# Two transformer layer pairs on one core: longer planned PSUM clears, more PSUM bank sets, and another instruction order

## The chip, the cores and the metric

The kernel runs on one core of one Trainium2 chip. TensorE (PE) multiplies matrices into PSUM, eight banks of 512 fp32 columns on 128 partitions. ScalarE (ACT), VectorE (DVE) and GpSimd (POOL) do the rest, the first two also reading PSUM. SyncE (SP) issues the DMAs. The metric is the device time of one execution in microseconds (us), the median of the runs.

## The reference

One sequence of 2048 tokens, width 512, bf16. Twice in a row, with the same weights, a sliding-window attention layer (32 heads of 16, window 256) and an MLP (512 to 1792 to 512, tanh GELU), each behind a layer norm and with a residual:

```python
def _A_ref(x, wqkv, wo):                       # H = 32, Dh = 16, W = 256
    q, k, v = split((x @ wqkv))                # 32 heads each
    scores = einsum("bhqd,bhkd->bhqk", q, k) * Dh ** -0.5
    mask = (i - j >= 0) & (i - j < W)
    p = softmax(where(mask, scores, -1e9))
    return einsum("bhqk,bhkd->bhqd", p, v) @ wo
def _B_ref(x, w1, b1, w2, b2):
    return gelu(x @ w1 + b1) @ w2 + b2

x = A_x
x = x + _A_ref(_layernorm(x), A_wqkv, A_wo)
x = x + _B_ref(_layernorm(x), B_w1, B_b1, B_w2, B_b2)
x = x + _A_ref(_layernorm(x), A_wqkv, A_wo)
x = x + _B_ref(_layernorm(x), B_w1, B_b1, B_w2, B_b2)
```

## The kernel before

The tokens are 16 tiles of 128; with the two layer pairs there are 32 tile steps (`tau`), grouped by two into 16 attention blocks (`b`) and by two or four into 10 MLP jobs (`J`). All of X and all weights stay in SBUF.

For a tile, `layernorm` takes statistics (`bn_stats`, `bn_aggr`, `veps` on VectorE), the inverse root (`rstd`, a power on GpSimd) and the normalised tile `xn` on VectorE. `xn` has to be transposed. Mostly TensorE does it into PSUM and VectorE or ScalarE copies it out (`xnTA`, `xnTB`). For the MLP's tiles 4 to 29 (`by_dma`) VectorE transposes 32x32 pieces into `xs_` (three buffers), four DMAs write them to a DRAM scratch (`scr_x`), and one DMA reads them back as `xnTB`.

For an attention block, 16-column groups of projections give Q, K and V; the K copy (`KT`) masks odd and even heads. A score visit (`sc`) puts 512 score columns of four row groups into four PSUM banks, two pairs; ScalarE takes the exponential of one pair at a time (128x1024) into the ring `E`. The triangles at the window's two edges are zeroed by a multiplication with `mask01`, on VectorE or GpSimd. A PV group (`pv`, pools name `od`) sums E times V in two banks; VectorE transposes, and divides by the sum of the exponentials (`TT`, `Rc`, `TM`, `OT`). `outproj` adds the result to X.

An MLP job multiplies by W1 into one bank at a time (pool `m1`, for the first six of 14 chunks `o`), applies GELU on ScalarE, and multiplies by W2 (`y`).

PSUM banks come from pools: each kind of user has a list of bank sets, and takes the one that is free first. At the start, 16 matmuls of zeros (`clear`, twice eight banks) precede every other use of PSUM. They read `gT`, which VectorE sets to zero first.

The order of all this isn't written in the program text. Every operation is a node with an engine, a duration, what it reads and writes, and perhaps a second engine that could do it. `ORDER` lists the 3295 nodes in the order in which they are recorded; a negative number picks the node's second engine. `_Plan.follow` walks the list with the nodes' durations, to choose the PSUM banks and to place the waits; each engine then runs its own nodes in that order. So a planned duration emits nothing, and changes only which banks are given out and where a wait stands. The one that the change touches is this:

```python
for h in range(NZ):
    PL.root = (add("pe", clear, 8 * mm(512), reads=["zero", "g0"], writes=["ps:init0", "ps:init1"], prio=-200, geo="f"),)
```

Lines of the profile: L32 and L36 are all matmuls and transposes of TensorE, L861 the memset of the zeros, L844 the reduction for `parmask`, L888 and L893 the loads of X and Wqkv, L933 to L943 the layer norm, L952 to L960 the way through DRAM, L916 and L918 the copies out of PSUM on VectorE and ScalarE, L990 the residual, L1030 the K copy, L1111 the exponential, L1132 the masks, L1197 to L1207 the end of a PV group, L1266 to L1278 the GELU.

Of the kernel before, what the change touches and what calls it, by code (L numbers as in the profile page):

```python
# [518 lines left out]
def bass_interleave_layers__sliding_block__dense_activation_gelu__prompt_kernel(  # L519
# [70 lines left out]
    def mm(n):  # L590
        return n / 2.4 + 2.6

    with ExitStack() as kctx:
        S_ = _Sched(nc, kctx)

        def sb(name, shape, dtype=dt.bfloat16):
# [33 lines left out]
        zero = gT[:, 0, :]  # L630
# [195 lines left out]
        add = PL.add  # L826
# [41 lines left out]
        for h in range(NZ):  # L868
            PL.root = (add("pe", clear, 8 * mm(512), reads=["zero", "g0"], writes=["ps:init0", "ps:init1"], prio=-200, geo="f"),)
# [450 lines left out]
        for i in order:  # L1320
            nd = PL.nodes[i]
            n = 1
            if nd["eng"] == "pe":
                c = _Count()
# [34 lines left out]
```

## Time and profile before

| | us |
|---|---|
| median of 3 runs (lowest, highest) | 461.64 (461.19, 461.93) |
| the profiled execution | 461.4 |
| its span, first to last instruction | 459.7 |
| PE busy | 442.2 |
| ACT busy | 394.2 |
| DVE busy | 370.0 |
| POOL busy | 216.5 |

The profile is of one execution. Its span is what the views divide; 1.7 us of the execution lie around it. The busy times overlap, as the engines run side by side; what ends the kernel is the chain of work in which each step waits for the one before. An idle time in a view has behind it what ended it.

### The profile page before, as it was taken

Reading aid. Unit: us, or ns where it says so; the run is one execution under the profiler, and the core shown is the slowest. Engines: PE = TensorE matmul, PEld = TensorE weight load, DVE = VectorE, ACT = ScalarE, POOL = GpSimd, SP = SyncE. Lnnn points to the kernel's source line nnn. Section 1 sums busy time; section 2 is a strip of 40 time slices with the busy share of each in tenths; the row PEclk is TensorE's granted clock in tenths of the full one; section 3 lists DMA queues with packets and bytes.
Section 4 is the critical chain, followed back from the end, with each engine's and each line's share of the span. In section 5 each row is a group of like instructions: output and inputs, shape, how many; then the busy total and the mean of one; then the engine's idle time right before and its main releaser. Section 6 shows DMA issues by size and latency. Waiting matters only on the chain.

```text
span 459.7 us, 19399 instructions
## 1 busy us (share of the span) xinstructions
PE 442.2 (96%) x8793; PEld 236.5 (51%) x8793; DVE 370.0 (81%) x754; ACT 394.2 (86%) x473; POOL 216.5 (47%) x250
## 2 busy tenths in 40 slices
PE   6987899999889999999999999999999999999997
PEld 3654465754444445555435545546454554454663
DVE  5999878989989688995879988988888968896312
ACT  2999999999989989899996999979997999875442
POOL 4466636712653555553667654462344415451600
PEclk9999999999999999999999999999999999999999
DMA  7670000001020110100030110101030021102011
GB/s 228 206 266 3 4 3 3 5 1 37 8 55 3 20 31 15 37 3 9 16 74 5 27 23 12 40 4 19 3 66 26 6 57 31 43 5 70 13 58 47
DMA packets 27855, 18.17 MB, mean 40 GB/s; under 512 B 15868, under 2 KB 27260, under 8 KB 27772
## 3 DMA queue, kind: packets, MB, share of 16 engines
q1 hardware_dynamic: 27772, 16.92, 13.8%
q8 instruction: 69, 1.13, 1.0%
q14 instruction: 14, 0.11, 0.1%
HBM read 11.41 MB, written 5.51 MB: 37 GB/s over the span
## 4 chain that ended last, share of the span: by engine, by line
PE 70%; ACT 23%; DVE 2%; SPq 1%; DMA 1%; POOL 1%; issue 1%; DVEq 0%; POOLq 0%
PE ps L32 69%; ACT E L1111 18%; ACT gT L1278 2%; PE ps L36 1%; SPq L956 1%; ACT gT L1269 1%; ACT L1111 1%; DMA scr_x<-xs_ 1%; ACT Va L918 1%; ACT QT L918 1%; DVE KT L1030 1%; DVE gT L1266 0%; DMA xnTB<-scr_x 0%; SPq L960 0%; DVE xs_ L952 0%
## 5 line engine op out<-in xcount | busy, mean ns | idle before, releaser
L1111 ACT ACTIVATE E<-ps 128x1024 bf16<-128x1024 f32 x304 | 287.0, 1046 | 26.9 <-PE ps L32 26.3
L1132 POOL TENSOR_TENSOR E<-E,mask 128x512 bf16<-128x512 bf16 (+1 forms) x120 | 125.5, 1059 | 121.6 <-DVE E L1132 43.3
L32 PE MATMUL ps<-W_sb,gT 128*128 128x512 bf16 x448 | 118.3, 380 | 0.0
L32 PE MATMUL ps<-xnTB,W_sb 128*128 128x512 bf16 (+1 forms) x560 | 116.0, 337 | 0.9 <-DMA xnTB<-scr_x 0.7
L990 DVE TENSOR_TENSOR X<-X,ps 128x512 bf16<-128x512 bf16 x64 | 43.5, 683 | 40.3 <-PE ps L32 39.3
L32 PEld LDWEIGHTS ps<-xnTB,W_sb 128*128 128x128 bf16 x560 | 51.2, 98 | 46.0 <-ACT E L1111 2.9
L32 PE MATMUL ps<-QT,KT 32*64 32x320 bf16 (+4 forms) x2976 | 65.4, 258 | 6.6 <-ACT E L1111 4.8
L32 PE MATMUL ps<-xnTA,Wqkv_sb 128*128 128x256 bf16 x512 | 70.1, 274 | 0.7 <-ACT E L1111 0.4
L1278 ACT ACTIVATE gT<-ps,b1T 128x512 bf16<-128x512 f32 (+1 forms) x92 | 48.8, 588 | 22.1 <-PE ps L32 21.6
L940 POOL TENSOR_TENSOR rstd<-veps,mhalf 128x1 f32<-128x1 f32 x64 | 36.5, 575 | 57.0 <-DVE veps L937 55.7
L32 PEld LDWEIGHTS ps<-W_sb,gT 128*128 128x128 bf16 x448 | 39.5, 98 | 42.7 <-issue 5.9
L1132 DVE TENSOR_TENSOR E<-E,mask 128x512 bf16<-128x512 bf16 (+1 forms) x142 | 57.5, 433 | 4.6 <-ACT E L1111 4.5
L32 PEld LDWEIGHTS ps<-xnTA,Wqkv_sb 128*128 128x128 bf16 x512 | 46.0, 98 | 19.3 <-issue 2.9
L32 PEld LDWEIGHTS ps<-QT,KT 32*64 32x64 bf16 x2976 | 27.6, 103 | 51.6 <-ACT E L1111 35.6
L32 PE MATMUL ps<-E,Va 64*17 64x128 bf16 (+3 forms) x3872 | 49.0, 229 | 2.0 <-ACT E L1111 0.7
L1197 DVE STREAM_TRANSPOSE TT<-ps 128x1024 f32<-128x1024 f32 x32 | 39.9, 1245 | 11.6 <-PE ps L32 11.0
L32 PEld LDWEIGHTS ps<-E,Va 64*17 64x17 bf16 x3872 | 39.3, 85 | 19.0 <-PE ps L32 5.4
L1241 POOL TENSOR_TENSOR X<-X,b2b 128x512 bf16<-128x512 bf16 x32 | 36.7, 1157 | 17.9 <-DVE xn L943 6.4
L933 DVE BATCH_NORM_STATS2 stat<-X 128x6 f32<-128x512 bf16 x64 | 43.4, 683 | 1.4 <-DMA X<-in_A_x_dram 0.7
L1030 DVE TENSOR_TENSOR KT<-ps,parmask 128x1024 bf16<-128x1024 f32 x32 | 38.4, 1211 | 3.9 <-PE ps L32 3.7
L1266 DVE TENSOR_SCALAR gT<-ps,b1T 128x512 bf16<-128x512 f32 (+1 forms) x48 | 31.8, 672 | 5.7 <-PE ps L32 5.3
L32 PE MATMUL ps<-Wqkv_sb,xnTA 128*128 128x512 bf16 x128 | 35.2, 381 | 0.2 <-ACT E L1111 0.2
(49 smaller groups left out, 325.2 us busy)
## 6 DMA issues: line engine op xcount, KB each, us to landing
W_sb<-in_B_w_dram SPq DMA_DIRECT2D x2, 1792.0 KB, 12.9
scr_x<-xs_ SPq DMA_DIRECT2D x104, 32.0 KB, 1.6
xnTB<-scr_x SPq DMA_DIRECT2D x26, 128.0 KB, 2.1
out_dram<-X SPq DMA_DIRECT2D x16, 128.0 KB, 1.8
Wqkv_sb<-in_A_wqkv_dram SPq DMA_DIRECT2D x3, 512.0 KB, 6.4
X<-in_A_x_dram SPq DMA_DIRECT2D x3, 512.0 KB, 4.8
X<-in_A_x_dram SPq DMA_DIRECT2D x2, 256.0 KB, 2.9
Wo_sb<-in_A_wo_dram SPq DMA_DIRECT2D x1, 512.0 KB, 6.4
```

The costliest lines, as they stand in the source:

```text
L32: return self.e.matmul(*a, **k)
L918: alt=() if kind not in ACT_OK and not boot else (("act", lambda e, B: e.activation(dst(B), src(B), AF.Copy, scale=1.0), d_act(n) + 14, 0. ...
L933: add("dve", lambda e, B: e.bn_stats(stat6[:, k6, :], X[:, t, :]), 590, reads=["X%d" % t], writes=["st%d" % k6], prio=prio)
L940: add("pool", lambda e, B: e.tensor_tensor(out=rstd[:, k : k + 1], in0=veps[:, k : k + 1], in1=mhalf[:], op=ALU.pow), 535, reads=["ve%d" % ...
L990: add("dve", lambda e, B: e.tensor_tensor(out=X[:, t, :], in0=X[:, t, :], in1=ps[:, B[g][0], :], op=ALU.add), d_psum(512), reads=["X%d" % ...
L1030: add("dve", lambda e, B, g=g, i=i: e.tensor_tensor(out=KT[:, kb, :, 2 * i : 2 * i + 2, :].rearrange("p a c q -> p a (c q)"), in0=ps[:, B[ ...
L1111: add("act", lambda e, B, g_=g_, gi=gi: e.activation(E[:, 2 * gi : 2 * gi + 2, e0 : e0 + 512], ps[:, B[g_][0] : B[g_][0] + 2, :], AF.Exp, ...
L1132: op = lambda e, B, Ew=Ew, Mw=Mw: e.tensor_tensor(out=Ew, in0=Ew, in1=Mw, op=ALU.mult)
L1197: add("dve", lambda e, B: e.transpose(TT[:, s].rearrange("p a c q d -> p (a c q d)"), ps[:, B[g][0] : B[g][0] + 2, :].rearrange("p a n -> ...
L1241: add("pool", lambda e, B: e.tensor_tensor(out=X[:, t, :], in0=X[:, t, :], in1=b2b[:], op=ALU.add), 1110, reads=["X%d" % t, "b2b"], writes ...
L1266: add("dve", lambda e, B, g=g, fc=fc: e.tensor_scalar(out=gT[:, fc, 0:M], in0=ps[:, B[g][0], 0:M], scalar1=b1T[:, fc : fc + 1], scalar2=No ...
L1278: add("act", lambda e, B, g=g, fc=fc: e.activation(gT[:, fc, 0:M], ps[:, B[g][0], 0:M], AF.Gelu_apprx_tanh, bias=b1T[:, fc : fc + 1], scal ...
```

## The change

Five things change in the text. The two clears are planned at 16 and 10 matmul lengths instead of 8 and 8. The score visits may take any two pairs of adjacent banks, also pairs that start at an odd bank; the PV groups likewise. The four writes to the DRAM scratch are planned at 2300 ns with 500 ns of queue instead of 2100 and 400. And `ORDER` is a new list of the same 3295 nodes.

In the new list VectorE's first node is the memset of the zeros, and the `parmask` reduction comes after the fourth `xn`; tile 1's layer norm stands ahead of tile 0's; the first K projection stands ahead of the first Q projection. Of the masks, 31 wide and 8 narrow ones go from VectorE to GpSimd (VectorE then has 91 and 12, GpSimd 127 and 32). One scaling `TM` also goes to GpSimd, and two transposed tiles are copied out by ScalarE instead of VectorE. In the queue of SyncE the four scratch writes of a tile mostly stand together. The numbers of matmuls, DMAs, exponentials and table loads stay.

```diff
         ORDER = [
-            0, 18, 1, 19, 2, 20, 8, 4, 5, 21, 6, 14, 7, 22, 15, 16, 9, 23, 33, 10, 24, 11, 40, 12, 34, 3, 41, 17, 35,
...
+            3276, 3077, 3277, 3278,
         ]
...
         PL = _Plan({
-            "sc": [(0, 1, 2, 3), (4, 5, 0, 1), (2, 3, 4, 5), (6, 7, 0, 1), (2, 3, 6, 7), (4, 5, 6, 7)],
+            "sc": [(0, 1, 2, 3), (4, 5, 0, 1), (2, 3, 4, 5), (6, 7, 0, 1), (2, 3, 6, 7), (4, 5, 6, 7)] + [
+                (a, a + 1, c, c + 1) for a in range(7) for c in range(a + 2, 7) if a % 2 or c % 2],
             "o": [(6,), (7,), (5,), (4,), (3,), (2,), (1,), (0,)],
-            "od": [(6, 7), (4, 5), (2, 3), (0, 1)],
+            "od": [(6, 7), (4, 5), (2, 3), (0, 1), (5, 6), (3, 4), (1, 2)],
...
         for h in range(NZ):
-            PL.root = (add("pe", clear, 8 * mm(512), reads=["zero", "g0"], writes=["ps:init0", "ps:init1"], prio=-200, geo="f"),)
+            PL.root = (add("pe", clear, (16 - 6 * h) * mm(512), reads=["zero", "g0"], writes=["ps:init0", "ps:init1"], prio=-200, geo="f"),)
...
-                        ["scr%d_%d" % (v, r)], reads=["xs%d" % z], prio=prio, dur=2100.0, issue=400.0)
+                        ["scr%d_%d" % (v, r)], reads=["xs%d" % z], prio=prio, dur=2300.0, issue=500.0)
```

356 rows, old and new, of the table ORDER are left out of this document.

## The prediction

> **What bounds the kernel now.** I read the page first, then the busy time by stretch, then the timeline of the places where TensorE stands still.
>
> ```profile
> span 459.7 us, 19399 instructions
> ## 1 busy us (share of the span) xinstructions
> PE 442.2 (96%) x8793; PEld 236.5 (51%) x8793; DVE 370.0 (81%) x754; ACT 394.2 (86%) x473; POOL 216.5 (47%) x250
> ...
> ## 4 chain that ended last, share of the span: by engine, by line
> PE 70%; ACT 23%; DVE 2%; SPq 1%; DMA 1%; POOL 1%; issue 1%; DVEq 0%; POOLq 0%
> ```
>
> TensorE is busy for 442.2 of 459.7 us, so all that an order can win back is the 17.5 us in which it idles. The change alters no matmul, so I take the 442.2 us as given. The chain says that ScalarE (23%) is the other bound. Where the idle time lies, the stretches show (columns: length, then busy us and instruction count of PE, weight load, DVE, ACT, POOL; clock; DMA):
>
> ```profile
> 0.00:20.00 20.00, 16.47 (x158) 9.46 (x159) 14.48 (x41) 10.53 (x15) 7.94 (x26) 1.00 0.62 199
> 20.00:40.00 20.00, 17.64 (x412) 10.23 (x410) 18.97 (x46) 19.44 (x25) 13.49 (x14) 1.00 0.58 205
> 40.00:60.00 20.00, 16.91 (x455) 10.53 (x455) 18.45 (x42) 19.91 (x23) 11.10 (x12) 1.00 0.01 3
> ...
> 120.00:140.00 20.00, 16.84 (x506) 9.04 (x504) 17.66 (x37) 18.11 (x21) 11.88 (x13) 1.00 0.17 36
> 140.00:160.00 20.00, 20.00 (x329) 9.46 (x314) 15.65 (x35) 19.68 (x24) 8.14 (x10) 1.00 0.05 9
> 220.00:240.00 20.00, 18.95 (x334) 8.03 (x333) 16.90 (x35) 18.79 (x21) 12.11 (x13) 1.00 0.24 52
> 240.00:260.00 20.00, 20.00 (x371) 10.55 (x369) 17.97 (x37) 16.07 (x19) 16.10 (x18) 1.00 0.01 3
> ```
>
> Idle time of TensorE is 3.53 us in the first stretch, 2.36 and 3.09 in the next two, 3.16 from 120 to 140, 1.05 from 220 to 240, nothing in the two others shown. From 20 to 60 us ScalarE is the bound (39.35 of 40 us busy): its exponentials run without a break, and TensorE has nothing else to do, since no MLP work is ready yet. So a microsecond won before 20 us is kept by ScalarE, and later by TensorE, unless something else takes it.
>
> **1. The start.** The line that plans the clears at 16 and 10 matmul lengths instead of 8 and 8 issues nothing; it only makes the planner keep the banks closed for longer. What moves is the order: the memset of the zeros is now VectorE's first instruction, ahead of the reduction that waits for GpSimd, and tile 1's layer norm runs whole before tile 0's.
>
> ```profile
> 1.76 1.57 SPq L893 DMA_DIRECT2D Wqkv_sb<-in_A_wqkv_dram  x3
> ...
> 2.62 0.27 DVE L861 MEMSET gT<- 128x256 uint32 x1
> ...
> 2.95 5.26 PE L32 MATMUL ps<-gT 128*128 128x512 bf16 x16 [2.95 <-DVE gT L861]
> ...
> 3.62 1.29 DVE L933 BATCH_NORM_STATS2 stat<-X 128x6 f32<-128x512 bf16 x2 [0.72 <-DMA X<-in_A_x_dram]
> ...
> 5.25 1.79 POOL L940 TENSOR_TENSOR rstd<-veps,mhalf 128x1 f32<-128x1 f32 x3 [0.89 <-DVE veps L937]
> ...
> 6.24 0.73 DVE L943 TENSOR_SCALAR xn<-X,statmv,rstd 128x512 bf16<-128x512 bf16 x2
> ...
> 8.05 0.61 PE L36 MATMUL ps<-ident,xn 128*128 128x128 bf16 x8
> ...
> 8.47 1.08 ACT L918 ACTIVATE xnTA<-ps 128x512 bf16<-128x512 bf16 x2 [6.41 <-PE ps L36]
> ...
> 9.61 1.26 PE L32 MATMUL ps<-xnTA,Wqkv_sb 128*128 128x256 bf16 x10
> ...
> 13.65 0.42 PE L32 MATMUL ps<-QT,KT 32*64 32x256 bf16 x16
> ...
> 14.14 1.94 ACT L1111 ACTIVATE E<-ps 128x1024 bf16<-128x1024 f32 x2
> ```
> ```profile
> Wqkv_sb<-in_A_wqkv_dram SPq DMA_DIRECT2D x3, 512.0 KB, 6.4
> ```
>
> Both normalised tiles are ready at 6.97 us, and the transposes start at 8.05, when the clears end: the clears are the late one, by 1.1 us. With the memset first it can run where the other engines begin (SyncE's and ScalarE's first instructions stand at 0.78), so the clears go from 1.1 to 1.1 + 5.26 = 6.4 us. Next late is the layer norm. The first X lands at 3.6 in any case; 0.65 (one of two statistics in 1.29), about 0.5 for the two small steps, 0.55 (one of three rstd in 1.79) and 0.4 (xn) put tile 1 at 5.9 and tile 0, one round behind, at 7.2. Transposes then end at 7.7 instead of 8.66, and the second copy on ScalarE ends near 8.3 instead of 9.55. The order now puts the K projection first, which needs the second weight part: issued at about 2.3 (second third of 1.57 from 1.76), landed 6.4 later, at 8.7. So the first projection starts at 8.8 instead of 9.61: the load, not the copy, is what is late next, and it takes back half a microsecond. From there to the first score visit stand four groups of 8 projections at 1.26/10 = 0.126, at most 1.0 us each, and a transpose of 0.3, which gives 12.6 to 13.1 against 13.65. I take 12.7, since the ten matmuls of the row overlap at their ends. First exponential: 13.2 against 14.14, **-0.9 us**, bounds -0.4 and -1.4.
>
> **2. 20 to 140 us.** The front is ScalarE's; the gain of part 1 is handed through. At 120 to 140 two chains end together, the exponentials and the activation layout that goes through DRAM for the third MLP job:
>
> ```profile
> 120.86 0.67 DVE L990 TENSOR_TENSOR X<-X,ps 128x512 bf16<-128x512 bf16 x1
> ...
> 124.94 4.36 SPq L956 DMA_DIRECT2D scr_x<-xs_  x8
> ...
> 129.41 1.42 SPq L960 DMA_DIRECT2D xnTB<-scr_x  x3
> ...
> 132.51 1.04 PE L32 MATMUL ps<-xnTB,W_sb 128*128 128x512 bf16 x4
> ...
> 134.88 2.33 PE L32 MATMUL ps<-xnTB,W_sb 128*128 128x512 bf16 x10
> ```
>
> Residual to MLP takes 11.65 us here. The eight scratch writes cost 4.36 us of queue, and the loads go at once behind them. In the new order the writes of one tile stand together, then the next tile's four, so the last tile's writes are not mixed with the earlier one's. The 0.6 us by which 4.36 exceeds eight writes of 0.47 (1.42 for three loads) is the most that falls away. On the ScalarE side the wider pools let 34 of 152 score visits and 2 of 32 PV groups take bank sets that the old lists did not have (counted over the planner's bank choices), so a visit can start when any two pairs are free; nothing is added for that, and ScalarE's idle time in these stretches, 0.65 us from 20 to 60 and 1.89 from 120 to 140, is all it can win. Both sides have to move for TensorE to move; I take a third of the 2.5 us, **-0.8 us**, bounds 0 and -2.5.
>
> **3. 220 to 240 us.**
>
> ```profile
> 220.34 0.69 DVE L990 TENSOR_TENSOR X<-X,ps 128x512 bf16<-128x512 bf16 x1 [0.34 <-PE ps L32]
> ...
> 225.61 5.60 SPq L956 DMA_DIRECT2D scr_x<-xs_  x9
> ...
> 230.81 0.71 DVE L952 STREAM_TRANSPOSE xs_<-xn 128x512 bf16<-128x512 bf16 x1 [0.83 <-DMA scr_x<-xs_]
> ...
> 239.67 0.61 PE L32 MATMUL ps<-xnTB,W_sb 128*128 128x512 bf16 x2 [0.66 <-DMA xnTB<-scr_x]
> ```
>
> The last transpose waits 0.83 us until an old scratch write has freed its buffer, because writes of three tiles are interleaved in the queue; at the end TensorE waits 0.66 us for the load. In the new order the four writes of the oldest tile go first (the change also plans each write at 500 instead of 400 ns of queue, which by itself issues nothing). Then the transpose is 0.8 us earlier, more than the 0.66. **-0.7 us**; bounds 0, if the write queue stalls anyway, and -1.0, the whole idle time there.
>
> **4. Masks move to GpSimd.** In the order 31 wide and 8 narrow masks go from VectorE to GpSimd, one scaling goes too, and two copies go from VectorE to ScalarE.
>
> ```profile
> L1132 POOL TENSOR_TENSOR E<-E,mask 128x512 bf16<-128x512 bf16 x96 | 109.9, 1157 | 104.4 <-ACT E L1111 36.8 <-DVE E L1132 33.7 <-DVE TM L1202 22.0
> L1132 DVE TENSOR_TENSOR E<-E,mask 128x512 bf16<-128x512 bf16 x122 | 52.6, 459 | 4.5 <-ACT E L1111 4.5
> ...
> L1132 POOL TENSOR_TENSOR E<-E,mask 128x256 bf16<-128x256 bf16 x24 | 15.7, 669 | 17.1 <-DVE E L1132 9.6 <-DVE TM L1202 5.3 <-DVE xn L943 1.4
> L1132 DVE TENSOR_TENSOR E<-E,mask 128x256 bf16<-128x256 bf16 x20 | 5.2, 277 | 0.0
> ```
>
> VectorE loses 31 x 0.459 + 8 x 0.277 = 16.4 us, GpSimd gains 31 x 1.157 + 8 x 0.669 = 41.2 us and stands at 258 of 457 us, 56%. Neither bounds the whole; each moved mask is 0.7 us later at its PV group. I count that as 0: between the score visit that feeds a mask and the PV group that reads it stands enough other TensorE work, as GpSimd's own idle time shows (104.4 us before the wide masks, ended mostly by ScalarE and VectorE, not by TensorE). Without that cover it would cost up to 0.7 us at each of 32 PV groups. Nor do I count a gain for VectorE's lighter load.
>
> **Sum.** -0.9 - 0.8 - 0.7 = -2.4 us on a span of 459.7. The profiled execution took 461.4 us, 1.7 us around its span; it lies 0.24 under the median of the three runs, 461.64. So 459.2 us for the median.
>
> **Rivals.** *The gain is swallowed.* The next X tiles, the weights of the MLP and the DRAM chain of part 2 hang on loads whose times don't move, and VectorE, 18.97 of 20 us busy from 20 to 40, could take over as bound there. Then only part 3 remains, 0 to -0.7: 461.2. For it: VectorE's share. Against it: the chain from 20 to 60 us lies on ScalarE.
>
> *The clock falls back.* Ten warm matmuls take 2.33 us, the sixteen clears 5.26 against 16 x 0.233 = 3.7: 1.5 us are lost in the first clears, as if half the speed held for about 3 us. With the clears ending at 6.4 and only 12 transposes before 8.8, TensorE is nearly idle for 2.4 us. If that set it back, the next 3 us would lose 1.5 us, and the sum is -2.4 + 1.5 = -0.9: 460.7. Against it: from 40 to 60 us it idles 3.09 of 20 us and the granted clock of the row stays 1.00, though no single gap there is that long.
> The Trainium skill (TensorE: Matmul & The Clock Gate, Part 1) says that the array starts at half rate, is released after a busy window of about 3.4 us and falls back after an idle one of the same length. By that rule the clears' slow part moves with them, and 2.4 us of thin work is just short of a fall; a free-running window, which it also states, leaves the chance open.
>
> *Slower: rstd queues behind masks.* GpSimd also computes every rstd, and with the masks moved up to one more wide mask (1.157 us) stands ahead of the last rstd of an MLP job. That decides where the layer norm's chain to the job's first matmul is longer than the TensorE work between, as at 239.67; GpSimd is already 16.10 of 20 us busy right behind that place. Four jobs begin in the TensorE-bound part: 4 x 1.157 = +4.6, on top of -2.4: 463.8. Against it: before, the last rstd of that job is not what VectorE waits for at 230.81.
>
> *More is won.* If ScalarE and TensorE interlock better in all of 20 to 140 us, the full 2.5 us of part 2 and 1.4 of part 1 come: -1.4 - 2.5 - 1.0 = -4.9, 456.7.
>
> The change could also fail to do what it says: the planned lengths add no instruction, so all its effect is in the order, and the order does start the memset first.
>
> **How the numbers follow.** Forecast 0.62, with its own range 457.7 to 460.5; more won 0.10; swallowed 0.11; clock 0.05; slower 0.12. A measurement here can tell 0.2%, 0.9 us. The forecast and the larger gain are faster: 0.72. Swallowed and clock are within 0.2% (460.7 is on the edge): 0.16. Slower 0.12. The range leaves out the slower case and half of the larger gain: 457.2 to 461.9.
>
> **What would show it.** In the profile after: clears from about 1.1 us, the first projection at 8.8, the first exponential near 13.2; TensorE idle under 2.6 us from 120 to 140 and near 0.3 from 220 to 240, with no wait on the xnTB load; the page with VectorE at about 353 and GpSimd at about 258 us, TensorE still at 442. Wrong would be: projections after 8.8 us that take twice as long (clock), a TensorE wait for masks or for the xnTB load in the MLP jobs (queue on GpSimd), or the first exponential early and the stretch at 60 us no earlier than before (swallowed).

## The result, and the profile after

| us | before | changed |
|---|---|---|
| median of 6 runs (lowest, highest) | 461.85 (461.19, 462.8) | 459.84 (459.0, 460.33) |
| the profiled execution, its span | 461.4, 459.7 | 460.33, 458.5 |

By these medians the change is 2.0 us faster, where 2.4 was forecast. The ratio is 0.994, 95% interval 0.9921 to 0.9959, which is 1.9 to 3.6 us. Of the six runs of before, the three that the table ahead of the prediction doesn't have (462.5, 461.76, 462.8) are slower than the other three, and against their median the change gains 2.7 us. Run again, beside other runs of the kernel before, the ratio was 0.9945 (0.993 to 0.996), 2.4 us by the medians. The profiled execution of the changed kernel is the slowest of its six, 0.5 us over their median, and that of before lies 0.45 under its own. So the two profiles differ by 1.1 us only; the places are read from them, the sizes from the medians. Lines below 819 stand one further down in the changed kernel (L1111 is L1112).

The page, its busy times and the chain that ended last:

```profile
span 458.5 us, 19397 instructions
...
PE 442.5 (97%) x8793; PEld 235.6 (51%) x8793; DVE 362.1 (79%) x712; ACT 394.7 (86%) x475; POOL 257.6 (56%) x290
...
PE 71%; ACT 11%; DVE 9%; DMA 6%; SPq 2%; issue 1%; DVEq 0%
```

TensorE's work is what it was (442.5 us), so the whole gain is idle time, as the prediction had it. ScalarE's share of the chain fell from 23 to 11%; VectorE and the DMAs took its place. The busy time by stretch (columns as in the prediction):

```profile
0.00:20.00 20.00, 17.40 (x160) 9.73 (x160) 14.84 (x44) 11.12 (x15) 7.74 (x26) 1.00 0.61 194
20.00:40.00 20.00, 17.85 (x414) 10.34 (x413) 19.66 (x43) 19.64 (x24) 13.86 (x14) 1.00 0.60 209
40.00:60.00 20.00, 17.49 (x510) 11.24 (x514) 18.31 (x44) 19.90 (x23) 11.72 (x14) 1.00 0.01 3
120.00:140.00 20.00, 17.00 (x482) 8.98 (x480) 19.05 (x38) 17.40 (x20) 9.96 (x10) 1.00 0.14 30
220.00:240.00 20.00, 19.95 (x388) 8.82 (x380) 17.96 (x37) 19.57 (x23) 15.43 (x15) 1.00 0.18 43
```

TensorE idles 2.60 us in the first stretch (3.53 before), 2.15 and 2.51 in the next two (2.36, 3.09), 3.00 from 120 to 140 (3.16) and 0.05 from 220 to 240 (1.05). The timeline of the start:

```profile
0.91 0.27 DVE L862 MEMSET gT<- 128x256 uint32 x1 [0.91 <-PEq L1345]
...
1.23 5.61 PE L32 MATMUL ps<-gT 128*128 128x512 bf16 x16 [1.23 <-DVE gT L862]
...
6.68 0.73 PE L36 MATMUL ps<-ident,xn 128*128 128x128 bf16 x8
7.10 1.08 ACT L919 ACTIVATE xnTA<-ps 128x512 bf16<-128x512 bf16 x2 [5.04 <-PE ps L36]
...
9.12 1.03 PE L32 MATMUL ps<-xnTA,Wqkv_sb 128*128 128x256 bf16 x8 [0.54 <-DMA Wqkv_sb<-in_A_wqkv_dram]
...
12.93 0.42 PE L32 MATMUL ps<-QT,KT 32*64 32x256 bf16 x16
...
13.53 1.94 ACT L1112 ACTIVATE E<-ps 128x1024 bf16<-128x1024 f32 x2
```

The clears begin at 1.23, the copies are done at 8.18, and the first projection then waits 0.54 us for the K part of the weights. From there it takes 4.41 us to the first exponential. (In a second profile of the changed kernel, shown at the end of the experiments, that part lands later, and the first exponential stands at 14.36.) Behind it, ScalarE's own groups tell the next step; of before from 14.0 to 36.4 us, with the row that stands at the end of that stretch:

```profile
L1111 ACT ACTIVATE E<-ps 128x1024 bf16<-128x1024 f32 x21 | 20.2, 1073 | 0.6 <-PE ps L32 0.6
...
36.29 1.02 ACT L1111 ACTIVATE E<-ps 128x1024 bf16<-128x1024 f32 x1 [0.56 <-PE ps L32]
```

and of the changed kernel from 13.4 to 35.1 us:

```profile
L1112 ACT ACTIVATE E<-ps 128x1024 bf16<-128x1024 f32 x21 | 20.1, 1070 | 0.2
```

Before, ScalarE waited 0.56 us for a score visit; in the new order its first 21 exponentials have no such break, and one copy of Q fewer stands among them. Matched exponential by exponential, the first is 0.61 us earlier than before, the one at 36.29 is 1.34 earlier (34.95): this stretch gave 0.73, and gives the same in the second profile.

The third MLP job's way through DRAM, and the fifth's:

```profile
119.13 0.68 DVE L991 TENSOR_TENSOR X<-X,ps 128x512 bf16<-128x512 bf16 x1
122.83 4.80 SPq L957 DMA_DIRECT2D scr_x<-xs_  x8
127.79 1.38 SPq L961 DMA_DIRECT2D xnTB<-scr_x  x2
...
131.31 1.51 PE L32 MATMUL ps<-xnTB,W_sb 128*128 128x512 bf16 x6
```
```profile
229.30 0.71 DVE L953 STREAM_TRANSPOSE xs_<-xn 128x512 bf16<-128x512 bf16 x1
230.04 1.25 SPq L957 DMA_DIRECT2D scr_x<-xs_  x3
...
235.21 0.34 SPq L961 DMA_DIRECT2D xnTB<-scr_x  x1
...
237.69 1.04 PE L32 MATMUL ps<-xnTB,W_sb 128*128 128x512 bf16 x4
```

The third job starts 1.2 us earlier than before (131.31, 132.51), the fifth 2.0 (237.69, 239.67), and its transpose at 229.30 waits for no scratch write any more. At the eighth job 0.8 us are lost again: it starts 1.04 us earlier than before, and TensorE stands 0.54 us for xnTB (0.30 at the seventh).

### The profile page after: what moved, and what is told of

It reads as the page before. It is cut to its first block, busy times and chain, and to the rows that moved or that the text cites. A ratio compares the mean times of both kernels' runs of the same rounds, so it can differ in the third digit from the quotient of the medians.

```text
span 458.5 us, 19397 instructions
## 1 busy us (share of the span) xinstructions
PE 442.5 (97%) x8793; PEld 235.6 (51%) x8793; DVE 362.1 (79%) x712; ACT 394.7 (86%) x475; POOL 257.6 (56%) x290
## 4 chain that ended last, share of the span: by engine, by line
PE 71%; ACT 11%; DVE 9%; DMA 6%; SPq 2%; issue 1%; DVEq 0%
PE ps L32 70%; ACT E L1112 10%; DMA scr_x<-xs_ 2%; DMA xnTB<-scr_x 2%; DMA X<-in_A_x_dram 2%; DVE E L1133 1%; DVE stat L934 1%; PE ps L36 1%; SPq L957 1%; DVE KT L1031 1%; DVE Va L917 1%; DVE xn L944 1%; DVE xs_ L953 1%; ACT gT L1279 1%; DVE X L991 1%
## 5 line engine op out<-in xcount | busy, mean ns | idle before, releaser
L1112 ACT ACTIVATE E<-ps 128x1024 bf16<-128x1024 f32 x304 | 286.4, 1046 | 25.5 <-PE ps L32 24.6
L1133 POOL TENSOR_TENSOR E<-E,mask 128x512 bf16<-128x512 bf16 (+1 forms) x159 | 165.5, 1058 | 96.7 <-ACT E L1112 42.8
L1279 ACT ACTIVATE gT<-ps,b1T 128x512 bf16<-128x512 f32 (+1 forms) x92 | 48.7, 590 | 16.9 <-PE ps L32 16.4
L1133 DVE TENSOR_TENSOR E<-E,mask 128x512 bf16<-128x512 bf16 (+1 forms) x103 | 41.7, 432 | 6.7 <-ACT E L1112 6.3
```

The source lines that it names most:

```text
L1112: add("act", lambda e, B, g_=g_, gi=gi: e.activation(E[:, 2 * gi : 2 * gi + 2, e0 : e0 + 512], ps[:, B[g_][0] : B[g_][0] + 2, :], AF.Exp, ...
L1133: op = lambda e, B, Ew=Ew, Mw=Mw: e.tensor_tensor(out=Ew, in0=Ew, in1=Mw, op=ALU.mult)
L1279: add("act", lambda e, B, g=g, fc=fc: e.activation(gT[:, fc, 0:M], ps[:, B[g][0], 0:M], AF.Gelu_apprx_tanh, bias=b1T[:, fc : fc + 1], scal ...
```

## The experiments

Each set ran on one chip with its own runs of the kernel before; ratios are to those (462.72 median in the first set, 463.19 in the second, 462.59 in the third).

**The start alone** (the order of before):

```diff
-            0, 18, 1, 19, 2, 20, 8, 4, 5, 21, 6, 14, 7, 22, 15, 16, 9, 23, 33, 10, 24, 11, 40, 12, 34, 3, 41, 17, 35,
+            0, 18, 15, 1, 19, 2, 20, 8, 4, 5, 21, 6, 14, 7, 22, 16, 9, 23, 33, 10, 24, 11, 40, 12, 34, 3, 41, 17, 35,
...
-            PL.root = (add("pe", clear, 8 * mm(512), reads=["zero", "g0"], writes=["ps:init0", "ps:init1"], prio=-200, geo="f"),)
+            PL.root = (add("pe", clear, (16 - 6 * h) * mm(512), reads=["zero", "g0"], writes=["ps:init0", "ps:init1"], prio=-200, geo="f"),)
```

> The kernel before with one move: the memset of the zeros is VectorE's first node, ahead of the parmask reduction, and the clears are planned at 16 and 10 lengths. Theory (the start is handed through by ScalarE): clears from 1.2 us, first exponential at 13.3 to 13.6 us for 14.14, and the whole 0.6 to 0.9 us faster than before, 461.0 to 461.3. Rival (the next X tiles land at 11.5 to 11.9 us anyway and VectorE, which starts on them then, bounds the front): the first exponential is early, but the first MLP matmul stays at 53 us within 0.2 and the time within 0.3 of before.

Measured: 461.85 us, 0.9982 (0.9968 to 0.9996), 0.8 us. In its profile the first exponential stands at 13.17, 0.97 earlier than before. At the third MLP job most of it is held up:

```profile
132.43 1.04 PE L32 MATMUL ps<-xnTB,W_sb 128*128 128x512 bf16 x4 [0.63 <-DMA xnTB<-scr_x]
```

TensorE is there early and waits for the load, so that in this execution the job starts only 0.09 us earlier than before. The residual that feeds the load has moved with the front here too (120.15; 120.86 before). What is late is a scratch write: of the eight writes of this stage one stands much longer in the queue than the others, in the profile of before 1.16 us and here 1.60 (shortest, median and longest in ns, before and here):

```profile
L956 SPq DMA_DIRECT2D scr_x<-xs_ x8: 303/432/1157, 124.9 to 128.9; - x8
```
```profile
L956 SPq DMA_DIRECT2D scr_x<-xs_ x8: 303/432/1602, 124.2 to 128.6; - x8
```

Why one write takes longer stays open; in each of eleven profiles 7 to 11 of all 104 scratch writes stood over 1 us, with a median of 0.43. In the order of before, with its own engines, there are four profiles. This write took 1.16, 1.60, 1.82 and 1.87 us, and TensorE waited 0, 0.63, 1.12 and 0.84 us for the load, the last of these in the next experiment but one, whose front is that of before. So the profile of before, with no wait here, is the exception. In the new order 12.18 us lie between that residual and the job's first matmul (119.13 to 131.31), where before has 11.65. In none of its seven profiles with the new engines and bank lists does TensorE wait there, though the longest write takes up to 1.81 us.

**The changed kernel with the clears late** (`parmask` ahead of the memset again, both planned at 8):

```diff
-            0, 1, 2, 8, 4, 14, 15, 3, 5, 6, 9, 10, 11, 18, 40, 41, 42, 43, 19, 20, 21, 22, 23, 24, 33, 34, 44, 35, 84,
+            0, 1, 2, 8, 4, 14, 3, 5, 6, 7, 15, 9, 10, 11, 18, 40, 41, 42, 43, 19, 20, 21, 22, 23, 24, 33, 34, 44, 35,
...
```

> The changed kernel with the start undone: the parmask reduction and behind it the memset stand first on VectorE again, and the clears are planned at 8 and 8. Theory: clears from about 3 us, first exponential 0.6 to 1.0 us later than in the changed kernel, and the whole 0.6 to 1.0 us slower than it, 460.5 to 460.9. Rival (the gain is in the rest of the order): the time of the changed kernel within 0.3, 459.6 to 460.1.

Measured: 461.18 us, 0.996 (0.9942 to 0.9979). Against 0.994 and 0.9945 for the whole change, the early clears are worth 0.7 to 0.9 us in the new order too, by ratios whose intervals overlap. The run takes back more than the change gave: its clears start at 3.57, 0.62 later than before's, as `parmask` waits until 3.08 for `hot`, which GpSimd had ready at 2.46 in the order of before. Its first exponential comes 0.67 us later than before, the one that stood at 36.29 comes 0.06 earlier: again 0.73 from the order in between.

**The scratch writes of the fifth job alone** (the order of before; the oldest tile's writes 1323 and 1324 right behind 1322):

```diff
-            1450, -1604, 1321, -1427, 1451, 1452, 1489, 1453, 1438, 1208, 1463, 1325, 1480, 1454, 1595, 1322, 1416,
+            1450, -1604, 1321, -1427, 1451, 1452, 1489, 1453, 1438, 1208, 1463, 1325, 1480, 1454, 1595, 1322, 1323, 1324, 1416,
```

> The kernel before with two nodes moved: the four scratch writes of the tile at 206 us stand together and ahead of the next tiles' writes in SyncE's queue, as in the change. Theory of part 3: the transpose that waited 0.83 us for that tile's buffer waits no more, the fifth MLP job starts 0.5 to 0.7 us earlier than 239.67 and the whole is 0.5 to 0.7 us faster, 461.2 to 461.4. Rival (the chain to the job is VectorE's queue or the writes behind it): the job starts within 0.2 of before and the time is the same within 0.2.

Measured: 462.19 us, 0.9987 (0.9974 to 0.9999), 0.6 us. The stretch and the job's start in its trace:

```profile
220.00:240.00 20.00, 19.94 (x342) 8.68 (x340) 17.42 (x38) 19.12 (x21) 12.63 (x13) 1.00 0.22 48
```
```profile
230.36 0.71 DVE L952 STREAM_TRANSPOSE xs_<-xn 128x512 bf16<-128x512 bf16 x1
...
238.81 1.04 PE L32 MATMUL ps<-xnTB,W_sb 128*128 128x512 bf16 x4
```

The transpose no longer waits for a write, and idle time there falls from 1.05 to 0.06 us, without anything else of the change.

**Both parts together**, on the order of before (the two diffs above).

> The kernel before with both single parts that have been tried: memset first, parmask behind it, clears planned at 16 and 10, and the eight scratch writes of the fifth MLP job's last tiles in the order oldest tile first. Alone they gave 0.9982 and 0.9987. If they add up, 0.997, 1.4 us, and 0.6 us of the change's 2.0 are left to the rest of the order between 13 and 140 us. If the second only makes up for what the first leaves in that stretch (or the other way round), 0.998. If they are all of the change, 0.996 or lower.

Measured: 461.05 us, 0.9969 (0.9955 to 0.9982). They add up by the medians: 1.4 us. The profile of this kernel, its second slowest execution of twelve (462.19, median 461.05), shows neither: the third job starts at 132.56, after 1.12 us of waiting for its load, and the fifth at 239.26, after 0.78, though the transpose doesn't wait. So the sizes of these two parts are the medians' alone. In this set the changed kernel was at 460.15, so about 1 us is left for the rest of the order, of which the profiles show 0.73 between the first and the 21st exponential.

**The new order with the old bank lists.**

```diff
-            "sc": [(0, 1, 2, 3), (4, 5, 0, 1), (2, 3, 4, 5), (6, 7, 0, 1), (2, 3, 6, 7), (4, 5, 6, 7)] + [
-                (a, a + 1, c, c + 1) for a in range(7) for c in range(a + 2, 7) if a % 2 or c % 2],
+            "sc": [(0, 1, 2, 3), (4, 5, 0, 1), (2, 3, 4, 5), (6, 7, 0, 1), (2, 3, 6, 7), (4, 5, 6, 7)],
...
-            "od": [(6, 7), (4, 5), (2, 3), (0, 1), (5, 6), (3, 4), (1, 2)],
+            "od": [(6, 7), (4, 5), (2, 3), (0, 1)],
```

> The changed kernel with the old bank lists for score visits and PV groups; the order is the new one, and 367 of 675 groups get other banks. Theory (the wider lists let visits start when any two pairs are free): TensorE waits longer for ScalarE's release of banks, mostly between 20 and 140 us, and the whole is 0.5 to 1.5 us slower than the changed kernel. Rival (banks never decide): the same within 0.3.

Measured: 477.31 us, 1.032 (1.03 to 1.0339), some 17 us slower than the changed kernel, where 0.5 to 1.5 were expected. The waits (us in total, times, the longest):

```profile
PEld ps L32 <- ACT E L1111: 59.6, 124, 2.0
...
ACT E L1111 <- PE ps L32: 38.2, 49, 2.3
```

Before, the first was 45.4 us and the second 26.3 (46.7 and 24.6 in the changed kernel). 34 visits on new bank sets (31 by the planner's bank choices) looked like little; without them 367 of 675 groups get other banks, and TensorE and ScalarE each wait some 13 us longer for the other. The order needs the lists. The reverse, the wider lists in the order of before, changes none of the 675 choices, so it is the same program. What the new planned durations of the scratch writes do by themselves (other banks for 39 groups of the new order) no run shows.

**The masks as in the change, in the order of before** (75 masks to GpSimd, 36 to VectorE), and **as before, in the changed kernel's order** (the same flips back). One entry of the second kind, in the first of the two kernels:

```diff
-            129, -162, 120, 165, 121, 122, 253, 123, 951, -154, 254, 164, 183, 367, 958, 255, 256, 184, 368, 238, 124,
+            129, -162, 120, 165, 121, 122, 253, 123, 951, 153, 254, 164, 183, 367, 958, 255, 256, 184, 368, 238, 124,
```

> The kernel before, in its own order, with each mask on the engine that the changed kernel gives it: 75 go from VectorE to GpSimd and 36 from GpSimd to VectorE, net 39 to GpSimd; nothing else moves. Theory of the prediction: masks have cover on both engines, 0 within 0.5 us, ratio 0.999 to 1.001; GpSimd's busy time rises to about 258 us, VectorE's falls by 16. The rival (rstd and the PV groups queue behind masks on GpSimd): 2 to 4.6 us slower, ratio 1.004 to 1.010, with waits of VectorE for rstd or of TensorE for E by GpSimd in the MLP jobs. A third: the order was made for its own assignment, so that single masks come late wherever an order does not fit them, 1 to 3 us slower, spread over the run and not at the jobs.

> The changed kernel with each mask back on the engine that the kernel before gives it (75 to VectorE, 36 to GpSimd), in the changed kernel's order. Theory O (an order holds only with the engines that it was made for; the 4.6% that the same flips cost in the order before is misplacement on either engine): 1.03 to 1.05 of the kernel before here too, with TensorE waiting for E by GpSimd and by VectorE. Theory G (GpSimd's load is the cost: more masks there, later rstd and later PV groups; the new order merely hides it): no slower than the changed kernel, 0.992 to 0.995, since GpSimd has 39 masks less.

Measured: the first 483.98 us, 1.0456 (1.0424 to 1.0488); the second 518.94 us, 1.1235 (1.1211 to 1.126). The first's waits of ScalarE and of TensorE (26.3 and 0.5 us before):

```profile
ACT E L1111 <- PE ps L32: 40.1, 55, 2.4
...
PE ps L32 <- POOL E L1132: 3.8, 3, 2.5
```

And the second's, with its busy times:

```profile
PE 454.5 (88%) x8793; PEld 239.1 (46%) x8793; DVE 385.8 (75%) x751; ACT 399.6 (77%) x475; POOL 221.6 (43%) x251
...
ACT E L1112 <- PE ps L32: 66.6, 71, 4.0
...
PE ps L32 <- DVE OT L1208: 10.4, 5, 3.8
```

One place of the second kernel, where two masks wait 2.53 us for their exponentials and `OT` stands behind them:

```profile
304.83 1.58 DVE L1133 TENSOR_TENSOR E<-E,mask 128x512 bf16<-128x512 bf16 x2 [2.53 <-ACT E L1112]
306.33 0.70 DVE L1208 STREAM_TRANSPOSE OT<-TM 128x512 bf16<-128x512 bf16 x1
...
307.09 1.04 PE L32 MATMUL ps<-Wo_sb,OT 128*128 128x512 bf16 x4 [3.79 <-DVE OT L1208]
```

The kernel with the lighter GpSimd is the slowest of all, so GpSimd's load is not the cost. A mask on the wrong engine stands in that engine's queue where the list has it, and what is behind it comes late: masks on GpSimd in the first (TensorE waits 3.8 us for three of them), the last step of a PV group, `OT`, behind masks on VectorE in the second (10.4 us for five). TensorE being late then makes ScalarE wait, 40.1 and 66.6 us. So it is not load, and masks that stand wrongly in a queue are a cause that the traces show. How much of the price is theirs is not shown: with other engines the planner also gives other banks to 381 of 675 groups in the first kernel and to 517 in the second, and other banks alone cost 3% in the run above. No run separates the two. In the second, 12 us more are TensorE's own busy time (454.5 for 442.5), most of it by a lower clock (last section). The price, 12% where 3 to 5 were expected, was not foreseen.

**What bounds the front now.** The chain of the changed kernel hangs from 4.20 to 11.83 us on the landing of X's second group of tiles and then on VectorE. Three kernels change the loads alone; the last has both edits:

```diff
-        load_qkv(0)
         load_qkv(1)
+        load_qkv(0)
+        load_x(4, 4)
         load_qkv(2)
...
-        load_x(4, 4)
```

> The changed kernel, with the load of the K part of Wqkv issued ahead of the Q part; nothing else. In the changed kernel's trace the first projection starts at 9.12 us and has waited 0.54 us for that landing; the last statistics of the front wait 0.43 us for X4 until 11.85. Theory F (beyond 9 us the front hangs on X4's landing and on VectorE's chain behind it, as the chain of waits says): the first projection comes about 0.5 us earlier, the first exponential up to 0.5 earlier than 13.53, but the first MLP matmul stays at 52.0 within 0.2, and the time at the changed kernel's, 0.994 of the kernel before within 0.0007. Theory S (ScalarE's run of exponentials carries whatever comes earlier): the first MLP matmul 0.5 us earlier, the time 0.5 us lower, ratio 0.993.

> The changed kernel, with the load of X's second group of four tiles issued ahead of the third part of Wqkv; nothing else. It lands about 0.45 us sooner (one issue of 1.57/3 us), the V weights as much later. Theory F: VectorE's chain behind 11.85 moves by 0.3 to 0.45 us, the first MLP matmul too, time 0.3 to 0.45 lower than the changed kernel, ratio about 0.9932. Theory S: the first exponential stays at 13.5, the time too, ratio 0.994; a loss of up to 0.4 if the V projections then wait for their weights.

> The changed kernel with both edits of the loads: K part of Wqkv first, then Q, X's second group, V. Theory F: the two gains add, first exponential 0.5 us earlier, first MLP matmul 0.5 to 1.0 earlier, ratio 0.992. Theory S: as with the K part alone, 0.5 us, ratio 0.993. If a third thing bounds the front (the order of VectorE's own work), neither shows: 0.994.

Measured: K part first 460.3 us, 0.9935 (0.991 to 0.996); X early 459.95, 0.9932 (0.9907 to 0.9957); both 459.08, 0.9915 (0.9891 to 0.9939). In the order of the kernels, four rows, one and two:

```profile
8.42 1.04 PE L32 MATMUL ps<-xnTA,Wqkv_sb 128*128 128x256 bf16 x8
...
11.94 1.29 DVE L934 BATCH_NORM_STATS2 stat<-X 128x6 f32<-128x512 bf16 x2 [1.13 <-DMA X<-in_A_x_dram]
...
18.67 0.69 DVE L934 BATCH_NORM_STATS2 stat<-X 128x6 f32<-128x512 bf16 x1 [0.78 <-DMA X<-in_A_x_dram]
...
21.03 0.60 ACT L919 ACTIVATE Va<-ps 128x512 bf16<-128x512 f32 x1 [1.37 <-PE ps L32]
```
```profile
9.70 1.03 PE L32 MATMUL ps<-xnTA,Wqkv_sb 128*128 128x256 bf16 x8 [1.11 <-DMA Wqkv_sb<-in_A_wqkv_dram]
```
```profile
8.54 1.05 PE L32 MATMUL ps<-xnTA,Wqkv_sb 128*128 128x256 bf16 x8
...
10.77 1.28 DVE L934 BATCH_NORM_STATS2 stat<-X 128x6 f32<-128x512 bf16 x2
```

With the K part first the first exponential comes at 12.88, but VectorE waits longer for X and ScalarE stands 1.37 us at 21.03: the first MLP job starts at 52.83, later than the changed kernel's 52.01. The chain leads from that wait back to X's third group of tiles, for which VectorE waits until 18.67. X's groups of four tiles took a median of 6.3 us to land in this execution and 4.9 in the changed kernel's; whether the edit made them slower isn't shown. With X early alone the weights are late (1.11 us). With both neither waits, and the first exponential (12.96), the first MLP matmul (51.44) and the third job (130.73) are 0.57 or 0.58 us earlier. So neither theory holds by itself: ScalarE carries the front as long as X is there in time, and with the weights early X is what it lacked in this execution. Singly neither edit stands out from the changed kernel by more than the interval.

**Both loads, and the queue at the eighth job** (the scratch write 2776 ahead of the load 2763), beside **the changed kernel again**.

```diff
-            2778, 2763, 2776, 2518, 2780,
+            2778, 2776, 2763, 2518, 2780,
```

> The changed kernel with K part of Wqkv first, X's second group ahead of the V part, and in SyncE's queue the first scratch write of the eighth job's last tile ahead of the load of the tile before it. The two loads gave 0.9915 alone. If the queue at 387 us is what makes TensorE wait 0.54 us at 394 in the changed kernel: up to 0.5 us more, 0.9905. If the wait came from single slow writes (the trace with both loads has no such wait): 0.9915, 0.25% under the changed kernel in the same set.

> The changed kernel as it is, on the same chip as the three others of this set, so that they are compared with it directly. All theories: 0.994 of the kernel before, within 0.0015. Its place at 394 us, where TensorE waited 0.54 us for xnTB, may or may not show again.

Measured: 459.21 us (458.81 to 459.41), 0.9925 (0.9912 to 0.9938), against 460.15 (459.15 to 460.87), 0.9945 (0.993 to 0.996), on the same chip. The loads' version is 0.9 us under the changed kernel by the medians, though the intervals overlap by a hair. The queue edit adds nothing to both loads (0.9915 there). And the wait at 394 us did not show again in the changed kernel's second profile, so it belongs to that execution. In this profile the front was another late one:

```profile
9.96 1.03 PE L32 MATMUL ps<-xnTA,Wqkv_sb 128*128 128x256 bf16 x8 [1.21 <-DMA Wqkv_sb<-in_A_wqkv_dram]
...
14.36 1.02 ACT L1112 ACTIVATE E<-ps 128x1024 bf16<-128x1024 f32 x1
```

So the first exponential is 0.22 us later here than in the profile of before, where it was 0.61 earlier in the first. The landing of the weights varies from one execution to the next (a median of 6.7 us from issue in the first profile, 7.5 in this one), and the changed kernel waits for it each time; the version with the K part first does not.

## Why the prediction was right

The sum fits: 2.4 us was forecast, and 2.0 to 2.7 were measured. Its first and third terms were right by their mechanism, the second by luck.

**1. The start, -0.9.** By the medians it held: 0.8 by the start alone, and 0.7 to 0.9 by its loss, which undoes more than was gained. Single executions don't show it: the first exponential is 0.61 us earlier in one profile of the changed kernel, 0.22 later in the other. The links held: the K part of the weights is late next, and 4.41 us from the first projection to the first exponential were worked out as 4.4. The first projection had it at 9.12 in one profile and at 9.96 in the other, instead of 8.8, so what that load takes back was put too low. The clears took 5.61 us instead of 5.26, which hid behind that load. The terms of the layer norm add up to 5.7 us, not the 5.9 that the prediction has for tile 1; the profile has tile 1 ready at 5.77 and tile 0 at 6.95.

**2. From 20 to 140 us, -0.8.** The sum is near (0.73 by the first 21 exponentials, of which 0.6 are left at the third job), but the number is luck. A third of 2.5 us was a guess, and 1.89 of the 2.5 lay from 120 to 140 us, where nothing came: TensorE's idle time there is 3.00, not under 2.6, and ScalarE's grew to 2.60. The 0.6 us of the third job's way through DRAM were put down to mixed writes. The mixing cost nothing: one of the eight writes took 1.16 us and the others 0.30 to 0.44, and in the new order one takes 1.36 (4.80 us for all, 4.36 before). The gain came from the smaller part that the prediction names, ScalarE's idle time from 20 to 60 us, of which one wait for a score visit (0.56 of 0.65) went. What the prediction missed is that the third job's load is mostly late in the order of before (0.63 to 1.12 us in three of four profiles). The front's gain is handed on at that job because the new order leaves half a microsecond more between the residual and the job, which was not forecast.

**3. From 220 to 240 us, -0.7.** The mechanism held: in five profiles with the writes together the transpose waits for none of them. The size held by the median of the writes alone, 0.6, with an interval that ends at 0.9999, and in the first profile, which gains 0.9 from the fourth to the fifth job and has 0.05 of idle time instead of 0.3. That TensorE would not wait for the load held there only: in the second profile it waits 0.31 us, with both parts alone 0.78.

**4. The masks, 0.** The number holds for the whole, the reason fell. Idle time of GpSimd was taken as cover; but the same assignment in the order of before leaves GpSimd just as idle and costs 21 us. The cover is not in the engine's free time but in where the order puts each mask, and in the banks that were chosen with it. The busy times by form, after:

```profile
L1133 POOL TENSOR_TENSOR E<-E,mask 128x512 bf16<-128x512 bf16 x127 | 144.9, 1157 | 83.0 <-ACT E L1112 37.8 <-DVE E L1133 24.0 <-DVE xn L944 9.7
...
L1133 DVE TENSOR_TENSOR E<-E,mask 128x512 bf16<-128x512 bf16 x91 | 38.5, 450 | 2.8 <-ACT E L1112 2.3
```

GpSimd is at 257.6 us as worked out (258). VectorE's masks lost 15.9 us, near the 16.4, yet the page has 362.1 and not 353: the 64 `xn` take 443 instead of 398 ns (2.9 us more), and the sum over all groups falls by 12.2, of which the page, where overlapping instructions count once, shows 7.9. That step was mis-sized; nothing hangs on it.

**The rivals.** *Swallowed* did not happen: the first MLP matmul is 1.07 us earlier in the first profile (52.01, 53.08 before) and 0.24 in the second (52.84), and the medians keep the gain. *rstd behind masks on GpSimd* does not occur: VectorE's `xn` wait 3.2 us for rstd in all, 4.8 before. The sign that was named for it, a wait of TensorE for xnTB in the MLP jobs, did show at the seventh and eighth job (0.30 and 0.54 us), but the chain there runs over the scratch writes and the load, with no work of GpSimd. *The clock falls back* did not happen here, and did at eight places within three of the experiments (below). *More is won* did not happen, as 456.7 was not reached; by the medians 0.9 us can still be had at the front by moving both loads.

## What to carry to other kernels

In a list that fixes each engine's queue, an engine's idle time is no cover for an operation moved to it: order, engines and bank lists were made together here. The engines of one order in the other cost 4.6 and 12%, the old bank lists in the new order 3%, and the wider lists in the old order change nothing, while the whole gained 0.6%. A gain at the front is worth what the next load or DRAM round lets through; look for the first later place where the engine that carries the gain already waits for a transfer. Where two loads are each late by about half a microsecond, moving one shows little, so both have to be tried together. And a wait that one profile has or lacks can be one transfer that was slow that time: at the third job the profile that the prediction was read from had none, and three others of its order had 0.6 to 1.1 us.

## What the runs showed of the hardware

**The clock falls back after a window that is half busy, not only after an idle one.** In the traces' clock records every length at full or half speed that the end doesn't cut is a multiple of 3.413 us, so that windows of that length follow each other without regard to the work. Two windows of the kernel with the masks as in the change, in the order of before, and two of the one with the masks back (columns as above; the clock is third from the end):

```profile
138.48:141.89 3.41, 1.62 (x31) 0.49 (x28) 2.13 (x4) 3.41 (x4) 0.66 (x1) 1.00 0.41 115
141.89:145.30 3.41, 3.41 (x93) 1.87 (x93) 1.75 (x4) 1.65 (x3) 2.16 (x2) 0.50 0.02 5
```
```profile
407.09:410.50 3.41, 1.12 (x74) 0.77 (x55) 3.34 (x6) 0.23 (x1) 0.48 (x1) 1.00 0.02 5
410.50:413.91 3.41, 3.41 (x77) 2.40 (x74) 0.97 (x4) 2.79 (x4) 0.66 (x1) 0.50 0.00 0
```

TensorE was busy for 1.62 and 1.12 of 3.41 us, its longest single gap in the first being 1.14 us, and the next window ran at 0.50. Over the ten traces that have such records, twelve windows at full speed were followed by half speed, with 0.86 to 1.63 us of work in them; the least work in a window that was not is 1.65. So the line lies near 1.6 of 3.41 us; the ends of matmuls are modelled in the profile, so no finer. The way up needs more: at half speed windows with up to 2.58 us of work stayed there, those with 2.72 and more were followed by full speed. In the kernel with the masks back six windows within the run, 20.5 us, ran at half speed, which is up to 10 of the 12 us by which TensorE's busy time grew (442.5 to 454.5).
The Trainium skill (TensorE: Matmul & The Clock Gate, Part 1) gives a free-running window of 3413 ns, which agrees, and a fall after at least one idle window, which is too lenient if idle means without work: here a little under half busy was idle enough. In the changed kernel no window before the end came under the line, and by either rule nothing is lost there.

**The clears' length is a matter of phase.** Sixteen clears took 4.96 us with the start alone, 5.61 in the changed kernel and 6.24 in the new order with the old bank lists, all from 1.23 or 1.24 us on; the first full-speed record stands 2.7, 4.1 and 5.3 us behind their start, and each of these times ends a window of 3.413 us. The window in which the clears begin holds 2.72, 0.63 and 1.92 us of their work, and by the figures above only the first is enough. The changed kernel alone has clears of 5.61 and 5.35 us in its two profiles, so a few tenths in the start are not the kernel's.

**A normalisation on VectorE became slower with the order**: `xn` 398 ns in the order of before, 443 in the new one, 490 in the order of before with the change's masks. It is 443 with the masks back too, so the number of masks on GpSimd is not what sets it; the cause stays open.
